# Twenty small loads in the middle of a cached-attention decode kernel: sixteen on GpSimd's queue, four on SP's

## The chip, the cores and the metric

The kernel runs on one core of one Trainium2 chip. The metric is the device time of one execution in microseconds (us). The engines are PE (TensorE), DVE (VectorE), ACT (ScalarE), POOL (GpSimd) and SP (SyncE, which only issues DMAs here). Transfers issued by SP, ACT and POOL are carried by the core's 16 DMA engines.

## The reference

Everything is fp32. One new token for each of two batch rows attends over a cache of 4096 keys and values in 16 heads of 256; beside it a small feed-forward network runs on the same token, and a gate mixes the two:

```python
g = sigmoid((x * gate_w).sum(-1, keepdims=True))      # x: (2, 1, 448)
q = (x @ wq).reshape(B, 1, 16, 256).transpose(0, 2, 1, 3)
p = softmax(einsum("bhqd,bhkd->bhqk", q, k_cache) * 256 ** -0.5)
a = einsum("bhqk,bhkd->bhqd", p, v_cache).transpose(0, 2, 1, 3).reshape(B, 1, 4096) @ wo
h = relu(x @ w1 + b1)
b = (h * h) @ w2 + b2                                  # w1: (448, 1792)
return g * a + (1 - g) * b
```

The two caches, 2 x 16 x 4096 x 256 x 4 B = 134 MB each, are nearly all of the data.

## The kernel before

The attention is cut into 16 rounds (`rounds`, L258): a round is two heads of one batch row. For a round, K and V come as 128 partitions of 64 rows of 256, 8.39 MB each (`of_round`, L264): a partition holds 64 consecutive keys of one head.

**Buffers.** K has two tiles, `kp0` and `kp1`, used in turn by round (`load_k`, L268). V has one, `vp` (`load_v`, L272). All three also take other things at other times: `wq` and `w1` pass through `vp` at the start, the output weights `wo` through `kp` after each group of four rounds (`load_wo`, L514), and `w2` through `kp1` at the end.

**A round's work.** DVE multiplies the K tile in place by the query (`times_q`, L399, recorded at L403) and sums each 256 (`row_sums`, L405, recorded at L408) into the scores `s0` or `s1`, in turn by round. `rest` (L411) does both for the two halves of the tile: product, sum, product, sum. `maximum` (L418) and `softmax` (L427) make the weights with DVE, PE and ACT. `values` (L465) multiplies them with V on PE into the PSUM tile `po0`. After four rounds `sums`, `norm`, `turn_wide` and `project` bring the group's output through `wo` into `acc`.

**Order.** The program is written out by hand as one list of operations. `Flow.op` (L46) takes, with every operation, the regions that it reads (`r`) and writes (`w`), and puts it at the end of its engine's queue. An operation that reads a region waits for the last that wrote it; one that writes a region waits for those that wrote or read it before. A wait that is already implied by what the engine has waited for is left out (`know`). A DMA counts on a semaphore of its own name, stands in the queue of the engine that issues it, and counts as having read or written its regions when it has landed. An engine works its queue in order, so a wait holds all that stands behind it on that engine.

`load` (L251) records a DMA. Thus SP's queue in round i is: V of round i (waits until `values(i - 1)` has read `vp`), then K of round i + 2 (waits until DVE has summed the K tile of round i), and, after each fourth round, `wo`. The main loop is at L575 to L600:

```python
for i in range(LOOPED):          # LOOPED = 12
    ...
    vt = load_v(i, vp)
    if i < last - 3 - 1 or i + 2 < 14:
        load_k(i + 2)
    values(i, vt)
    clear(i)
    rest(i + 1, 0, 0)
    ...
    maximum(i + 1, True)
    softmax(i + 1)
```

Rounds 12 to 15 follow, written out one by one (L602 to L650), then the last products with `wo` and `w2` into `fin` (L652 to L655), a copy by ACT (L657) and the two stores (L659, L660). At the end SP clears the kernel's semaphores (L168).

POOL makes the identity matrix at the start (L298, L299) and a few constants, and issues no DMA. ACT issues four small loads at the start (L291 to L294) and one of the two stores.

Of the kernel before, what the change touches and what calls it, by code (L numbers as in the profile page):

```python
# [10 lines left out]
PE, ACT, DVE, POOL, SP = "PE", "ACT", "DVE", "POOL", "SP"  # L11
# [159 lines left out]
def gated_mix_kernel(nc, x, k_cache, v_cache, wq, wo, w1, b1, w2, b2, gate_w, out):  # L171
    P = 128
    B, H, S, DH = k_cache.shape
# [30 lines left out]
    def sb(name, *shape):  # L204
        return nc.alloc_sbuf_tensor(name, shape, F32).ap()
# [42 lines left out]
    def rows(t):  # L248
        return t.rearrange("p (j d) -> p j d", d=DH)

    def load(eng, sem, dst, src, w, r=(), give=None):  # L251
        e = flow.eng[eng]
        op(eng, lambda: e.dma_start(dst, src), r=r, w=w, dma=sem, give=give)

    def place(t, lo=0, hi=NK * DH):
        return ("vp" if t is vp else "kp1" if t is kp[1] else "kp0", lo, hi)
# [7 lines left out]
    def of_round(src, i):  # L264
        b, n = rounds[i]
        return src[b, 2 * n:2 * n + 2].rearrange("h (p j) d -> (h p) j d", p=PH)

    def load_k(i, lo=0, hi=NK):  # L268
        t = kp[i % 2]
        load(SP, f"k{i % 2}_{lo}", rows(t)[:, lo:hi, :], of_round(k_cache, i)[:, lo:hi, :], [place(t, lo * DH, hi * DH)])  # L270

    def load_v(i, t, cuts=()):  # L272
        at = [0, *cuts, NK]
        for lo, hi in zip(at, at[1:]):
            give = "v" if i < LOOPED else None
            load(SP, "v" if give else f"v{i}_{lo}", rows(t)[:, lo:hi, :], of_round(v_cache, i)[:, lo:hi, :],
                 [place(t, lo * DH, hi * DH)], give=give)
        return t
# [50 lines left out]
    def mms(calls):  # L329
        def run():  # L330
            for out_, lhsT, rhs, start, stop in calls:
                i = t_.matmul(out_, lhsT, rhs, start=start, stop=stop, skip_group_check=True)  # L332
            return i
        return run

    op(PE, mms([(pxv[:, c, :], xr[:, c].rearrange("b r s -> b (r s)"), ident[:B, :B], True, True) for c in range(XC)]),
       r=[xr_r, "ident"], w=["sm"])
# [35 lines left out]
    def make_q(i, token=False):  # L373
        c = sel if token else col(i)
        op(PE, mms([(pq[k * PH:(k + 1) * PH, :DH], c.to_broadcast([P, PH]), qs[:, k * DH:(k + 1) * DH], True, True)
                    for k in range(2)]), r=["qs", "sel" if token else "ident"], w=["pq"], take=["q"] if token else ())
        t = q_t[i % 3]
        q_of[i] = t
        op(ACT, lambda: s_.activation(t, pq[:, :DH], AF.Copy), r=["pq"], w=[f"q{i % 3}"])  # L379

    def pick(i):
        c = col(i)
        op(ACT, lambda: s_.activation(sel, c, AF.Copy), r=["ident"], w=["sel"], give="q")
# [10 lines left out]
    for k in range(FB // 2):  # L394
        op(ACT, lambda k=k: s_.activation(h_sb[:, k * D:(k + 1) * D], ph[32 * k:32 * k + 2 * B, :D], AF.Copy),
           r=["ph"], w=[("shared", k * D, (k + 1) * D)])
    load_k(1)

    def times_q(i, half, lo, hi):  # L399
        t, a, q = kp[i % 2], half * J, q_of[i]  # L400
        kt = rows(t)[:, a + lo:a + hi, :]
        at = [place(t, (a + lo) * DH, (a + hi) * DH)]
        vec(lambda: v_.tensor_tensor(kt, kt, q.unsqueeze(1).to_broadcast([P, hi - lo, DH]), op=ALU.mult), at + [f"q{i % 3}"], at)  # L403

    def row_sums(i, half):  # L405
        t, s = kp[i % 2], s_t[i % 2]
        at = slice(half * J, (half + 1) * J)
        vec(lambda: v_.tensor_reduce(s[:, at], rows(t)[:, at, :], axis=AX.X, op=ALU.add),  # L408
            [place(t, half * HALF, (half + 1) * HALF)], [(f"s{i % 2}", half, half + 1)])

    def rest(i, first, lead):  # L411
        if lead < J:
            times_q(i, first, lead, J)
        row_sums(i, first)
        times_q(i, 1 - first, 0, J)
        row_sums(i, 1 - first)

    def maximum(i, token=False):  # L418
        s = s_t[i % 2]
        vec(lambda: v_.tensor_reduce(m, s, axis=AX.X, op=ALU.max), [f"s{i % 2}"], ["m"], give="m" if token else None)  # L420
        op(PE, mms([(mt[k * PH:(k + 1) * PH, :PH], m.to_broadcast([P, PH]), ident[:, k * PH:(k + 1) * PH], True, True)
                    for k in range(2)]), r=["m", "ident"], w=["mt"], take=["m"] if token else ())

    def buf(i):
        return 0 if i <= LOOPED else i % 2

    def softmax(i):  # L427
        b, n = rounds[i]
        s, nb, rs, pw = s_t[i % 2], nb_t[i % 2], None, pwt[buf(i)]
        vec(lambda: v_.tensor_reduce(nb, mt[:, :PH], axis=AX.X, op=ALU.max, negate=True), ["mt"], [f"nb{i % 2}"])  # L430
        u, k = unit_of[2 * n]
        rs = rs_t[u % 2]

        def part(e):
            at = slice(e * PH, (e + 1) * PH)
            c = B * (k + e) + b
            op(ACT, lambda: s_.activation(pw[at, :, 2 * c:2 * c + 2], s[at].rearrange("p (m s) -> p m s", s=2), AF.Exp,  # L437
                                          bias=nb[at], accum_out=rs[at, c:c + 1]),
               r=[f"s{i % 2}", f"nb{i % 2}"], w=[(f"pw{buf(i)}", 2 * c, 2 * c + 2), (f"rs{u % 2}", c, c + 1)],
               give="pw" if e and i < LOOPED else None)  # L440

        part(0)
        part(1)

    def clear(i):
        b, n = rounds[i]
        u, k = unit_of[2 * n]
        at = pwt[0].rearrange("p m (k b s) -> p m k b s", b=B, s=2)[:, :, k:k + 2, b, :]
        op(ACT, lambda: s_.activation(at, zero.unsqueeze(2).unsqueeze(3).to_broadcast([P, NK // 2, 2, 2]), AF.Copy), r=["zero"],  # L449
           w=[("pw0", 2 * (B * (k + e) + b), 2 * (B * (k + e) + b) + 2) for e in range(2)])  # L450

    def sums(u):
        n = B * len(units[u])
        op(PE, mms([(sm[:, :n], ones_pp, rs_t[u % 2][:, :n], True, True)]), r=["ones", f"rs{u % 2}"], w=["sm"])
# [10 lines left out]
    def values(i, vt, lo=0, hi=NK // 2):  # L465
        b, h = rounds[i]
        u, k = unit_of[2 * h]
        n = len(units[u])
        po, pw = po_t[u % 2 if u > 2 else 0], pwt[buf(i)]
        name = f"po{u % 2 if u > 2 else 0}"  # L470
        token = i < LOOPED
        calls = []
        for mm in range(lo, hi):
            r = 32 * (mm % 4)
            calls.append((po[r:r + 4 * n, :], pw[:, mm, :4 * n], vt[:, 2 * mm * DH:(2 * mm + 2) * DH],
                          not token and k == 0 and b == 0 and mm < 4,
                          token or (k == n - 2 and b == B - 1 and mm >= NK // 2 - 4)))
        op(PE, mms(calls), r=[f"pw{buf(i)}", place(vt, 2 * lo * DH, 2 * hi * DH)], w=[name], take=["pw", "v"] if token else ())
# [35 lines left out]
    def load_wo(u, i):  # L514
        t = kp[i % 2]
        tv = t[:, :HJ * D]
        if u < NG - 1:
            load(SP, "wo", tv, wo_g[u], [place(t, 0, HJ * D)])
        else:
            load(SP, "wo3", tv.rearrange("p (h k) -> p h k", h=HG), wo_v[:, u * HG:(u + 1) * HG, :], [place(t, 0, HJ * D)])  # L520
# [38 lines left out]
    def ffn_square(pt):  # L559
        for a in range(2):  # L560
            at = slice(a * PH, (a + 1) * PH)
            vec(lambda a=a, at=at: v_.tensor_tensor(hb[at], pt[at, :, a * B:(a + 1) * B], b1T[at].unsqueeze(2).to_broadcast([PH, FC, B]),
                                         op=ALU.add), ["sm", "b1T"], [("hb", a, a + 1)])
        vec(lambda: v_.tensor_scalar(hb, hb, 0.0, None, op0=ALU.max), ["hb"], ["hb"])
        vec(lambda: v_.tensor_mul(hT, hb, hb), ["hb"], ["hT"])
        vec(lambda: v_.tensor_tensor(hT, hT, gP[:, 1, :].unsqueeze(1).to_broadcast([P, FC, B]), op=ALU.mult), ["hT", "gP"], ["hT"])
# [5 lines left out]
    make_q(2)  # L572
    pick(3)

    for i in range(LOOPED):  # L575
        if i % HG == 0:
            flow.loop()
        flow.next_pass()
        vt = load_v(i, vp)
        if i < last - 3 - 1 or i + 2 < 14:  # L580
            load_k(i + 2)
        values(i, vt)
        clear(i)
        rest(i + 1, 0, 0)
        if i == 0:
            ffn_square(pt)
        if i % HG == HG - 1:
            load_wo(i // HG, i + 1)
        maximum(i + 1, True)
        softmax(i + 1)  # L590
        make_q(i + 3, True)
        if i < LOOPED - 1:
            pick(i + 4)
        if i % HG == HG - 1:
            u = i // HG
            flow.end_loop(16 * u)
            sums(u)
            norm(u)
            turn_wide(u)
            project(u)  # L600

    i = last - 3  # L602
# [16 lines left out]
    i = last - 2  # L619
# [13 lines left out]
    i = last - 1  # L633
# [55 lines left out]
```

## Time and profile before

| | us |
|---|---|
| median of 3 runs | 678.31 (678.14 to 678.61) |
| the profiled execution | 678.43 |
| its span, first to last instruction | 677.1 |
| DVE busy | 569.6 (84%) |
| PE busy, matmuls | 246.3 (36%) |
| PE busy, weight loads | 83.3 (12%) |
| ACT busy | 42.6 (6%) |
| POOL busy | 0.7 (6 instructions) |

Times inside the profile are counted from the span's start. The page cuts the span into 40 equal slices and gives for each the busy tenths of the DMA engines and what they moved. Queues are numbered: q1 is fed by SP, q10 by ACT, q8 and q14 fetch instructions. A row of a group gives line, engine, operation, output and input, count, then busy time and mean ns of one, then the idle time just before them and what ended it. SPq is SP's queue of DMA issues; the time of such a row is that of issuing, not of the transfer.

### The profile page before, as it was taken

To read this page: it belongs to the slowest core of one execution; us is meant where nothing else is said; L and a number is where in the kernel's file an instruction comes from. 1 tells how busy PE (TensorE), PEld (TensorE's weight loads), DVE (VectorE), ACT (ScalarE), POOL (GpSimd) and SP (SyncE) were. 2 spreads that over 40 slices of the span, in tenths; PEclk is the share of its full clock that TensorE was granted. 3 is DMA by queue.
4 is the path that set the end of the run, shared out by engine and by line. 5 is a ranking of instruction groups with operands and counts; after the bars stand their busy time and mean duration, and the time that the engine had idled before them with its cause. 6 is when DMAs were issued, how large, how long until landed. Compare 5 with 4: busy or idle time off the path is not lost.

```text
span 677.1 us, 3790 instructions
## 1 busy us (share of the span) xinstructions
PE 246.3 (36%) x1658; PEld 83.3 (12%) x1658; DVE 569.6 (84%) x141; ACT 42.6 (6%) x142; POOL 0.7 (0%) x6
## 2 busy tenths in 40 slices
PE   2522350502306751140505455040411580602486
PEld 1100210100101510010101411010100240100122
DVE  3069999999999895979979896997979899999920
ACT  0001000000100201010000201000010110100000
POOL 0000000000000000000000000000000000000000
PEclk9957575665757566575856578585565865855789
DMA  9999999999999999999999999999999999999997
GB/s 380 434 430 435 435 434 434 434 434 434 434 434 434 451 434 434 434 434 434 434 434 434 430 431 434 434 434 434 434 434 434 406 451 422 432 443 434 401 429 299
DMA packets 7622, 289.71 MB, mean 428 GB/s; under 512 B 950, under 2 KB 1084, under 8 KB 2364
## 3 DMA queue, kind: packets, MB, share of 16 engines
q1 hardware_dynamic: 7448, 289.54, 99.2%
q8 instruction: 8, 0.13, 0.1%
q10 hardware_dynamic: 164, 0.02, 0.0%
q14 instruction: 2, 0.02, 0.0%
HBM read 289.56 MB, written 0.00 MB: 428 GB/s over the span
## 4 chain that ended last, share of the span: by engine, by line
DVE 41%; DMA 36%; PE 0%; issue 0%; ACT 0%; DVEq 0%
DMA kp<-in_A_k_cache_dram 32%; DVE s L408 21%; DVE kp L403 20%; DMA kp<-in_B_w_dram 4%; PE fin L332 0%; PE mt L332 0%; DVE nb L430 0%; ACT shared L657 0%; DVE rc L460 0%; DVE rl L461 0%; DVE rc L459 0%; DVE m L420 0%; DVEq L147 0%
## 5 line engine op out<-in xcount | busy, mean ns | idle before, releaser
L403 DVE TENSOR_TENSOR kp<-kp,q 128x8192 f32<-128x8192 f32 (+2 forms) x34 | 278.2, 8182 | 57.3 <-DMA kp<-in_A_k_cache_dram 57.3
L408 DVE TENSOR_REDUCE s<-kp 128x32 f32<-128x8192 f32 x32 | 277.9, 8686 | 1.1
L332 PE MATMUL po<-vp,pw 128*16 128x512 f32 (+1 forms) x960 | 138.8, 736 | 223.9 <-PEq L145 207.1
L332 PEld LDWEIGHTS po<-vp,pw 128*16 128x16 f32 (+1 forms) x960 | 31.1, 111 | 327.4 <-issue 306.4
L332 PE MATMUL mt<-ident,m 128*64 128x64 f32 x64 | 7.3, 318 | 148.9 <-PEq L145 85.5
L332 PE MATMUL sm<-rl,shared 128*128 128x8 f32 (+1 forms) x112 | 23.6, 347 | 9.1 <-ACT shared L488 8.1
L332 PE MATMUL acc<-kp,oTw 128*2 128x448 f32 x48 | 24.3, 673 | 2.5 <-ACT oTw L497 2.5
L332 PEld LDWEIGHTS mt<-ident,m 128*64 128x64 f32 x64 | 4.8, 191 | 162.9 <-issue 97.4
L449 ACT ACTIVATE pw<-zero 128x128 f32<-128x128 f32 x12 | 3.7, 311 | 326.9 <-PE po L332 326.9
L332 PEld LDWEIGHTS sm<-rl,shared 128*128 128x128 f32 x112 | 23.0, 311 | 10.7 <-DVE rl L461 4.6
L437 ACT ACTIVATE pw<-s,nb 64x64 f32<-64x64 f32 x32 | 11.1, 348 | 176.7 <-DVE nb L430 176.5
L332 PE MATMUL ph<-vp,xT 128*4 128x448 f32 x28 | 7.2, 679 | 16.6 <-DMA vp<-in_B_w_dram 16.6
L332 PE MATMUL po<-kp,pw 128*8 128x512 f32 x64 | 10.1, 790 | 8.1 <-DMA kp<-in_A_v_cache_dram 8.1
L430 DVE TENSOR_REDUCE nb<-mt 128x1 f32<-128x64 f32 x16 | 3.6, 223 | 11.1 <-PE mt L332 11.1
L332 PE MATMUL pq<-qs,sel 128*64 128x256 f32 x48 | 12.3, 594 | 0.0
L332 PE MATMUL po<-vp,xT 128*4 128x512 f32 x56 | 7.7, 711 | 4.9 <-DMA vp<-in_A_wq_dram 4.9
L459 DVE RECIPROCAL rc<-sm 128x8 f32<-128x8 f32 (+1 forms) x5 | 1.0, 196 | 7.9 <-PE sm L332 7.9
L488 ACT ACTIVATE shared<-po 128x512 f32<-128x512 f32 x12 | 6.5, 591 | 11.4 <-PE sm L332 11.4
L379 ACT ACTIVATE q<-pq 128x256 f32<-128x256 f32 x16 | 6.1, 384 | 13.1 <-PE pq L332 12.8
L332 PEld LDWEIGHTS acc<-kp,oTw 128*2 128x2 f32 x48 | 4.5, 98 | 20.1 <-issue 17.3
L437 ACT ACTIVATION_READ_ACCUMULATOR pw<-s,nb 64x1 f32 x32 | 5.9, 185 | 0.0
L332 PEld LDWEIGHTS pq<-qs,sel 128*64 128x64 f32 x48 | 4.1, 212 | 0.0
(64 smaller groups left out, 61.9 us busy)
## 6 DMA issues: line engine op xcount, KB each, us to landing
kp<-in_A_k_cache_dram SPq DMA_DIRECT2D x4, 4096.0 KB, 27.5
vp<-in_A_wq_dram SPq DMA_DIRECT2D x1, 7168.0 KB, 19.7
kp<-in_A_wo_dram SPq DMA_DIRECT2D x4, 1792.0 KB, 25.5
vp<-in_A_v_cache_dram SPq DMA_DIRECT2D x1, 4096.0 KB, 24.1
vp<-in_B_w_dram SPq DMA_DIRECT2D x1, 3136.0 KB, 19.0
vp<-in_A_v_cache_dram SPq DMA_DIRECT2D x1, 2048.0 KB, 28.6
kp<-in_B_w_dram SPq DMA_DIRECT2D x2, 896.0 KB, 29.9
vp<-in_A_v_cache_dram SPq DMA_DIRECT2D x1, 1024.0 KB, 30.6
```

The source lines that it names most:

```text
L332: i = t_.matmul(out_, lhsT, rhs, start=start, stop=stop, skip_group_check=True)
L379: op(ACT, lambda: s_.activation(t, pq[:, :DH], AF.Copy), r=["pq"], w=[f"q{i % 3}"])
L403: vec(lambda: v_.tensor_tensor(kt, kt, q.unsqueeze(1).to_broadcast([P, hi - lo, DH]), op=ALU.mult), at + [f"q{i % 3}"], at)
L408: vec(lambda: v_.tensor_reduce(s[:, at], rows(t)[:, at, :], axis=AX.X, op=ALU.add), [place(t, half * HALF, (half + 1) * HALF)], [(f"s{i % ...
L430: vec(lambda: v_.tensor_reduce(nb, mt[:, :PH], axis=AX.X, op=ALU.max, negate=True), ["mt"], [f"nb{i % 2}"])
L437: op(ACT, lambda: s_.activation(pw[at, :, 2 * c:2 * c + 2], s[at].rearrange("p (m s) -> p m s", s=2), AF.Exp, bias=nb[at], accum_out=rs[at ...
L449: op(ACT, lambda: s_.activation(at, zero.unsqueeze(2).unsqueeze(3).to_broadcast([P, NK // 2, 2, 2]), AF.Copy), r=["zero"], w=[("pw0", 2 * ...
L459: vec(lambda: v_.reciprocal(c, sm[:, :B * n].rearrange("p (k b) -> p k b", b=B)), ["sm"], ["rc"])
L488: op(ACT, lambda s=s, lo=lo: s_.activation(o_w[:, s], pv[:, s, lo:lo + HJ // 2].unsqueeze(2).to_broadcast([P, HJ // 2, HG, HP]), AF.Copy), ...
```

## The change

Two spare tiles of 8 partitions by 4 x 256 elements are allocated, one for SP's small loads and one for POOL's. A new function `few` loads the first `k` partitions' first four rows of a round's K cache, `k` rows of 4 KB, into the spare tile, and names the scores of that round as read. In the rounds 2 to 9 POOL issues two such loads of one row; in the rounds 4 to 7 SP issues one of 1, 2, 4 and 8 rows, right after the K load of round i + 2. Nothing reads the spare tiles. Each load has a semaphore of its own. Since all loads of one engine write the same tile, each waits until the one before it has landed; since they name the scores as read, the sum that next writes those scores (round i + 2, or i + 3 for the loads called `two`) waits until they have landed. [...]

```diff
+    spare = {e: sb(f"spare{e}", 8, 4 * DH) for e in (SP, POOL)}
+
+    def few(eng, name, k, i):
+        load(eng, name, spare[eng][:k], of_round(k_cache, i)[:k, :4, :].rearrange("p j d -> p (j d)"), [f"spare{eng}"],
+             r=[f"s{i % 2}"])
+
     for i in range(LOOPED):
         if i % HG == 0:
             flow.loop()
@@
         vt = load_v(i, vp)
         if i < last - 3 - 1 or i + 2 < 14:
             load_k(i + 2)
+        if 2 <= i < 10:
+            few(POOL, f"one{i}", 1, i)
+        if 4 <= i < 8:
+            few(SP, f"few{i}", 1 << i - 4, i)
         values(i, vt)
         clear(i)
         rest(i + 1, 0, 0)
+        if 2 <= i < 10:
+            few(POOL, f"two{i}", 1, i + 1)
         if i == 0:
             ffn_square(pt)
@@
-    nc = _bacc.Bacc("TRN2", target_bir_lowering=False, num_devices=1)
+    nc = _bacc.Bacc("TRN2", target_bir_lowering=False, num_devices=1, dynamic_dma_scratch_size=8192)
```

## The prediction

> **What bounds the kernel now.** I read the page's slices and queues first, because the loads added are DMA work. In the slices each digit is a fortieth of the span.
>
> ```profile
> span 677.1 us, 3790 instructions
> DMA  9999999999999999999999999999999999999997
> GB/s 380 434 430 435 435 434 434 434 434 434 434 434 434 451 434 434 434 434 434 434 434 434 430 431 434 434 434 434 434 434 434 406 451 422 432 443 434 401 429 299
> DMA packets 7622, 289.71 MB, mean 428 GB/s; under 512 B 950, under 2 KB 1084, under 8 KB 2364
> q1 hardware_dynamic: 7448, 289.54, 99.2%
> q8 instruction: 8, 0.13, 0.1%
> q10 hardware_dynamic: 164, 0.02, 0.0%
> ```
>
> The 16 DMA engines are busy from start to end, and q1, which SP feeds, takes 99.2% of them. Slice after slice moves 434 GB/s; a sixteenth of that, 27.1 GB/s, is one engine's rate. 289.71 MB at 434 GB/s are 667.5 us of the 677.1. So the kernel is a DMA queue that never runs dry: whatever adds time to the DMA engines adds it to the end, and whatever delays another engine adds nothing until SP issues so late that the queue empties.
>
> How full is the queue? First the issues (KB each if alike, median us from issue to landing), then SP's own order, the K-cache and V-cache loads around the rounds that the change touches.
>
> ```profile
> kp<-in_A_k_cache_dram SPq DMA_DIRECT2D x14, 39.3
> vp<-in_A_v_cache_dram SPq DMA_DIRECT2D x14, 29.6
> ```
>
> ```profile
> 212.61 0.33 SPq L253 DMA_DIRECT2D vp<-in_A_v_cache_dram  x1
> 239.60 0.33 SPq L253 DMA_DIRECT2D kp<-in_A_k_cache_dram  x1
> 256.40 0.33 SPq L253 DMA_DIRECT2D vp<-in_A_v_cache_dram  x1
> 257.13 0.33 SPq L253 DMA_DIRECT2D kp<-in_A_k_cache_dram  x1
> 294.53 0.33 SPq L253 DMA_DIRECT2D vp<-in_A_v_cache_dram  x1
> 300.33 0.33 SPq L253 DMA_DIRECT2D kp<-in_A_k_cache_dram  x1
> 332.66 0.33 SPq L253 DMA_DIRECT2D vp<-in_A_v_cache_dram  x1
> ```
>
> A round's K or V is 2 heads x 4096 x 256 x 4 B = 8.39 MB, 19.3 us at 434 GB/s. A K load lands 39.3 us after its issue, so some 20 us of other loads are ahead of it; a V load has 10 us ahead.
>
> VectorE (DVE) is the second engine. Its rows, and its order in one stretch:
>
> ```profile
> L403 DVE TENSOR_TENSOR kp<-kp,q 128x8192 f32<-128x8192 f32 (+2 forms) x34 | 278.2, 8182 | 57.3 <-DMA kp<-in_A_k_cache_dram 57.3
> L408 DVE TENSOR_REDUCE s<-kp 128x32 f32<-128x8192 f32 x32 | 277.9, 8686 | 1.1
> ```
>
> ```profile
> 182.73 0.22 DVE L420 TENSOR_REDUCE m<-s 128x1 f32<-128x64 f32 x1
> 231.09 8.69 DVE L408 TENSOR_REDUCE s<-kp 128x32 f32<-128x8192 f32 x1
> 257.13 0.22 DVE L420 TENSOR_REDUCE m<-s 128x1 f32<-128x64 f32 x1
> 265.57 8.69 DVE L403 TENSOR_TENSOR kp<-kp,q 128x8192 f32<-128x8192 f32 x1 [7.47 <-DMA kp<-in_A_k_cache_dram]
> 274.30 8.69 DVE L408 TENSOR_REDUCE s<-kp 128x32 f32<-128x8192 f32 x1
> 304.34 8.69 DVE L403 TENSOR_TENSOR kp<-kp,q 128x8192 f32<-128x8192 f32 x1 [2.90 <-DMA kp<-in_A_k_cache_dram]
> ```
>
> ```profile
> DVE 41%; DMA 36%; PE 0%; issue 0%; ACT 0%; DVEq 0%
> ```
>
> A round is four operations of 8.7 us and waits for its K load: 7.47 us before round 6, 2.90 before round 7. The chain of waits puts 41% of the span on DVE and 36% on DMA, but it follows semaphores: it names DVE because DVE frees the K buffer, while the engines behind q1 were moving an earlier load. The full DMA row decides.
>
> **The change part by part.** Nothing is removed. Added are twenty loads with twenty semaphores of their own, 16 x 1 + 1 + 2 + 4 + 8 = 31 rows of 4 KB, 127 KB, which is 0.29 us at 434 GB/s if it spreads evenly. [...]
>
> *What a small packet costs a busy engine.* At the start ACT's b1 load (128 rows of 56 B) ran between the 57,344 B pieces of wq on q1. The stretch from 2.5 to 19.5 us (40 slices of 0.425 us; packets stand at their starts), then the one from 670 to 677 (slices of 0.175 us):
>
> ```profile
> GB/s 270 0 0 0 944 1079 135 0 0 945 1089 135 0 0 945 1080 135 0 0 945 1089 135 0 0 945 1080 135 0 0 945 1080 135 0 0 945 1080 135 0 0 1081
> q10 hardware_dynamic: 111, 0.01, 0.5%
> ```
>
> ```profile
> DMA  8898999999675544411000000000000000000000
> q10 hardware_dynamic: 8, 0.00, 0.1%
> ```
>
> 111 packets took 0.5% of 16 x 17 us = 272 us, so 12 ns each; the 8 of the end 0.1% of 112 us, 14 ns. And they leave no gap beside themselves: with some 7 of them on each engine, the bursts of wq come every 5 slices, 2.125 us, and a burst looks like the one before. A piece of 57,344 B at 27.1 GB/s takes 2.116 us. So changing between two queues costs a packet's own time, some 10 ns, and no more. I price a short packet at 16 ns (12 to 14 rounded up, since 256 B are more than 56 B: 256 B at 27.1 GB/s are 9 ns), and a 4 KB packet at 4096 / 27.1 = 151 ns plus 16 ns for its completion, 167 ns.
>
> *The sixteen loads of GpSimd.* No row of before has a load on GpSimd's queue, and none has a load of one row. From the lower side, a row that goes whole to one engine and to another engine each time puts one load on each: 0.17 us. From the upper side, whole rows always on the same engine put 16 x 167 ns = 2.7 us on it. Between them, a row cut in 16 pieces of 256 B puts two short packets, data and completion, on each engine: 16 x 2 x 16 ns = 0.51 us on all of them. I take 0.51: a contiguous row can be cut anywhere, and it lies nearer to the lower end, where the price comes from rows. [...]
>
> *The four loads of SP.* The 164 packets of q10 are 2 + 2 + 2 + 128 + 4 = 138 rows of ACT's five loads, and the 26 left over are 2 + 2 + 2 + 16 + 4: a load of k rows, k under 16, has k completions, so k engines. Then the loads of 2, 4 and 8 rows put 167 ns a row on as many engines: 3 x 167 = 0.50 us on an engine that is in all three, nothing on one in none, and 14 x 167 / 16 = 0.15 on the average. The load of one row is 0.03 cut in pieces, 0.17 whole. Issuing costs SP 0.33 us each, as its rows show, in stretches in which it waits tens of us.
>
> *Who sets the end.* The DMA row of the end falls from 9 to 1 over some 2 us: the engines finish that far apart, because each has carried its own share of instruction fetches (q8). After the last landing nothing changes:
>
> ```profile
> 673.71 0.95 PE L332 MATMUL fin<-kp,hT 128*2 128x112 f32 x32 [0.67 <-DMA kp<-in_B_w_dram]
> 674.72 0.26 ACT L657 ACTIVATE shared<-fin 128x112 f32<-128x112 f32 x1 [5.03 <-PE fin L332]
> 675.01 0.64 SPq L253 DMA_DIRECT2D out_dram<-shared  x1
> ```
>
> If the last engine carries none of SP's rows, the end moves by GpSimd's part alone.
>
> *The waits, all covered.* (1) SP's second to fourth small load wait for the one before to land (the same spare tile), which is behind a K load in q1. At i = 5 SP has issued K of round 7 at 257.13 and then stands until that of round 6 has landed, about 265.6; queued behind it on SP is V of round 6, due at 294.53, so 29 us are left. At i = 6 it stands from 300.7 to about 304.3, and V of round 7 is due at 332.66. The wait for the scores is no wait: the K load just ahead on SP has already waited for that sum. If this cover were gone, a delay D would cost D less the loads still queued: K at 239.60 landed by 265.57, 26.0 less 19.3, so 6.7 us are the thinnest cushion of this stretch. (2) DVE's first sum of round i + 2 overwrites the scores that the small loads name as read, so it waits for up to three landings. GpSimd's loads of round 3's scores are released at 182.7 and needed at 231.09: 48 us. SP's land right behind the K load of round i + 2, and the sum comes one product, 8.7 us, later. 274.30 comes 0.04 us after the end of the operation at 265.57, waits included; three more waits at that price are 0.12 us a round, and DVE idles 2.9 us or more for K in these rounds. (3) GpSimd has nothing else queued after its six instructions at the start.
>
> Sum: 0.51 + 0.03 + 0.15 = 0.7 us. The profiled execution took 678.43 us (span 677.1, 1.3 around it), 0.12 over the median of 678.31; so 679.1 from the one, 679.0 from the other. I predict **679.0**. The bounds of the unknown prices are 678.31 + 0.17 = 678.5 and 678.31 + 2.7 + 0.50 + 0.17 = 681.7.
>
> **The rivals.** *Rows whole on one engine (slower).* If a one-row load isn't cut, and GpSimd always begins at the same engine, that engine has 2.7 us of its own, plus 0.67 where it also carries SP's. Bulk loads are complete when their slowest engine is, and the end waits for it. It decides from the point at which the extra exceeds that engine's lead over the last one, at most the 2 us of the DMA row above. For it: ACT's two-row loads did use just two engines. Against it: nothing but that a contiguous row can be cut. It gives 681.0 to 681.7.
>
> *GpSimd's packets hold an engine longer (slower).* If those descriptors cost not 16 ns but 100, 32 of them on each engine are 3.2 us: 681.5. For it: no row shows that queue. Against it: q10, the other small queue, leaves no gap. A stronger form: a small load occupies all 16 engines for a fixed span, whatever its bytes. If a load held them for half a microsecond or more, 20 loads would be 10 us and above, 688 and later. The packets of q10 speak against it, since 111 of them took 1.4 us in all. [...]
>
> *A wait that isn't covered (slower).* A small load that lands 45 us late would hold DVE. Nothing in the rows comes near.
>
> [...]
>
> **How the numbers follow.** 0.2% is 1.36 us, about what a measurement of this kernel can tell from no change. Forecast, 678.2 to 679.6, within 0.2%: 0.65. Rows whole on one engine: 0.13. GpSimd's packets dearer: 0.12. Fixed span per load: 0.04. An uncovered wait: 0.03. Faster by over 0.2%: 0.03. So slower is 0.32, the same 0.65, faster 0.03. The range goes from 678.2 (the lower bound less the 0.3 by which runs of before spread) to 681.7, the upper bound; outside are the fixed span, the uncovered wait, the fast case and part of the dearer packets, under 0.2.
>
> **What would show it.** Right: a new queue with 16 x 32 = 512 packets, mostly under 512 B, at a share of 0.1% or less; the GB/s row still at 434; DVE's idle time before L408 unchanged; SP's V issues no later than before by more than the drift of under 1 us. If rows go whole, the new queue has some 4 KB packets and the DMA row of the end falls more slowly, one engine trailing. If GpSimd's packets are dearer, GB/s falls below 434 between 147 and 500 us, and nowhere else. A wait of DVE for a spare tile, or a gap in the DMA row, would make the whole argument wrong.

## The result, and the profile after

The changed kernel takes 682.33 us (median of 4 runs, 682.09 to 682.44) against 678.30: 4.0 us more, ratio 1.0059 with a 95% interval of 1.0047 to 1.0071. The profiled execution took 682.43 us. From its page: span, what each fortieth of it moved, the queues, and DVE's two large groups.

```profile
span 681.1 us, 3831 instructions
GB/s 378 466 423 444 440 435 431 431 431 431 431 424 408 453 431 428 435 432 431 431 433 431 449 432 431 427 435 431 431 435 431 416 444 421 431 445 435 406 419 225
q1 hardware_dynamic: 7478, 289.60, 98.7%
q0 software_dynamic: 512, 0.07, 0.1%
L403 DVE TENSOR_TENSOR kp<-kp,q 128x8192 f32<-128x8192 f32 (+2 forms) x34 | 278.2, 8183 | 61.8 <-DMA kp<-in_A_k_cache_dram 61.8
L408 DVE TENSOR_REDUCE s<-kp 128x32 f32<-128x8192 f32 x32 | 278.0, 8686 | 1.1
```

Much is as before. GpSimd's queue (q0) has 512 packets that take 0.1%; q1 has 30 packets more, 15 rows and 15 completions. DVE waits for no small load (the 1.1 us before L408 stand), only 4.5 us longer for K. So the K loads themselves land later. The last slice moves 225 GB/s in place of 299: something drains more slowly. The end shows it, cut in slices of 0.275 us from 670 to 681 us, first the kernel before, then the changed one:

```profile
GB/s 404 384 437 358 384 431 261 254 209 209 143 65 33 13 0 0 0 0 0 0 0 0 7 7 0 0 0 0 0 0 0 0 0 0 0 0 0 0 0 0
```

```profile
GB/s 437 417 417 417 391 372 450 358 235 319 222 215 248 117 52 26 26 26 86 26 39 20 20 39 20 20 26 26 0 0 0 0 0 0 0 0 0 7 7 0
```

27.1 GB/s, a sixteenth of the 434 of the full slices, is the rate of one DMA engine. Before, the rate falls from that of 16 engines to none within some 2 us. After, most engines end about half a microsecond later than before, and then 13 slices, 3.6 us, run at 20 to 39 GB/s (q8's one packet here, a 16 KB instruction fetch, makes the 86): **one engine works on alone.** The last product waits for it; before, the same row stood at 673.71:

```profile
677.69 0.95 PE L332 MATMUL fin<-kp,hT 128*2 128x112 f32 x32 [0.69 <-DMA kp<-in_B_w_dram]
```

SP's queue, in the stretch that the prediction showed, and its waits for small loads in all:

```profile
257.24 0.33 SPq L253 DMA_DIRECT2D kp<-in_A_k_cache_dram  x1
266.12 0.25 SPq L253 DMA_DIRECT2D spareSP<-in_A_k_cache_dram  x1
295.08 0.33 SPq L253 DMA_DIRECT2D vp<-in_A_v_cache_dram  x1
300.70 0.33 SPq L253 DMA_DIRECT2D kp<-in_A_k_cache_dram  x1
305.21 0.27 SPq L253 DMA_DIRECT2D spareSP<-in_A_k_cache_dram  x1
333.60 0.33 SPq L253 DMA_DIRECT2D vp<-in_A_v_cache_dram  x1
```

```profile
SPq L253 <- DMA spareSP<-in_A_k_cache_dram: 17.7, 3, 8.5
```

SP stands as predicted, 8.5 us at most, and the V loads follow when they did, later by 0.55 and 0.94 us, within the drift that was allowed.

### The profile page after: what moved, and what is told of

Same layout as the page of the kernel before. It is cut to its first block, busy times and chain, and to the rows that moved or that the text cites. A ratio compares the mean times of both kernels' runs of the same rounds, so it can differ in the third digit from the quotient of the medians.

```text
span 681.1 us, 3831 instructions
## 1 busy us (share of the span) xinstructions
PE 244.9 (36%) x1658; PEld 83.0 (12%) x1658; DVE 569.8 (84%) x141; ACT 42.6 (6%) x142; POOL 8.6 (1%) x22
## 4 chain that ended last, share of the span: by engine, by line
DVE 41%; DMA 37%; PE 0%; issue 0%; ACT 0%; DVEq 0%
DMA kp<-in_A_k_cache_dram 33%; DVE s L408 20%; DVE kp L403 20%; DMA kp<-in_B_w_dram 4%; PE fin L332 0%; PE mt L332 0%; DVE nb L430 0%; ACT shared L669 0%; DVE rc L460 0%; DVE rl L461 0%; DVE rc L459 0%; DVE m L420 0%; DVEq L147 0%
## 5 line engine op out<-in xcount | busy, mean ns | idle before, releaser
L408 DVE TENSOR_REDUCE s<-kp 128x32 f32<-128x8192 f32 x32 | 278.0, 8686 | 1.1
L332 PE MATMUL po<-vp,pw 128*16 128x512 f32 (+1 forms) x960 | 135.8, 722 | 232.0 <-PEq L145 215.5
L253 POOL DMA_DIRECT2D sparePOOL<-in_A_k_cache_dram x16 | 7.9, 493 | 455.0 <-DVE s L408 401.4
```

## The experiments

**Theory A**: the pieces of a row come from 16 engines and all land in one partition of SBUF; the engine that brings the bulk rows of that place is held, that is, its own packets take longer. **B**: the upkeep of GpSimd's queue holds one engine, whatever the data. **C**: SP's whole rows pile up on one engine. That a row's pieces come from sixteen engines is read off the packet records of the changed kernel: those of the first load start between 151.7 and 152.9 us, and their completions, taken in order, follow by 2.43 to 2.63 us. In between, sixteen bulk packets of 64 KB start, of 2.42 us each (median), so sixteen engines are at work at once. Times are medians; each is set against the runs of the kernel before that were made with it (678.3 to 678.4).

| kernel | us | over before | ratio, 95% interval |
|---|---|---|---|
| GpSimd's sixteen alone, partition 0 | 680.88 | 2.50 | 1.0020 to 1.0049 |
| SP's four alone | 678.95 | 0.57 | 0.9997 to 1.0017 |
| GpSimd's, 16 partitions in turn | 679.04 | 0.66 | 1.0000 to 1.0019 |
| GpSimd's, 256 B a row | 678.73 | 0.35 | 0.9995 to 1.0014 |
| GpSimd's, 8 KB a row | 683.00 | 4.62 | 1.0051 to 1.0085 |
| whole change, GpSimd's rows in partition 64 | 680.25 | 1.87 | 1.0017 to 1.0039 |
| GpSimd's, partitions 0-3 and 32-35 in turn | 680.73 | 2.35 | 1.0022 to 1.0047 |
| whole change, each row over 16 partitions | 679.58 | 1.20 | 1.0008 to 1.0027 |
| sixteen cut rows through SP, partition 0 | 680.64 | 2.30 | 1.0021 to 1.0046 |
| the same through GpSimd, no wait between loads | 680.76 | 2.42 | 1.0023 to 1.0048 |
| sixteen whole rows through SP, partition 0 | 679.41 | 1.07 | 1.0006 to 1.0025 |
| thirty-two through GpSimd, no wait between loads | 684.51 | 6.15 | 1.0074 to 1.0107 |

### Each part alone

```diff
-        if 4 <= i < 8:
-            few(SP, f"few{i}", 1 << i - 4, i)
```

> GpSimd's sixteen loads alone, SP's four left out. The changed kernel's trace shows one DMA engine trailing the others at the end, by 5.9 us where the last trailed by 2.2 before. Theory A (all pieces of a one-row load land in one partition of SBUF, and the engine that carries the bulk rows of that place is held, some 0.3 us a load): 681.6, with the trailing engine still there. Theory B (upkeep of GpSimd's queue holds one engine, whatever the data are): also 681.6. Theory C (SP's whole rows pile up on one engine): 678.8.

```diff
-        if 2 <= i < 10:
-            few(POOL, f"one{i}", 1, i)
...
-        if 2 <= i < 10:
-            few(POOL, f"two{i}", 1, i + 1)
```

> SP's four loads alone, GpSimd's sixteen left out. A and B: at most 0.7 us above before, 678.3 to 679.0, and no long trail at the end. C: 681.6 or more.

680.88 and 678.95. C falls as the main cause: SP's rows alone cost 0.57, hardly more than the runs spread. GpSimd's loads alone cost 0.7 us less than the 681.6 that A and B gave, but they leave the trail, from slice 14 to 22 of the same stretch (counted from 0):

```profile
GB/s 437 437 417 424 372 391 378 261 254 241 189 183 203 65 20 20 39 20 20 39 13 26 13 0 0 0 0 0 0 0 0 5 7 2 0 0 0 0 0 0
```

The parts make 2.50 + 0.57 = 3.1, together 4.0. That fits two delays of the same engine of which each, taken alone, is partly hidden by that engine's lead: the time by which it would have ended before the last engine. A and B are both still open.

### The place, and the bytes

```diff
-    spare = {e: sb(f"spare{e}", 8, 4 * DH) for e in (SP, POOL)}
+    spare = {SP: sb("spareSP", 8, 4 * DH), POOL: sb("sparePOOL", P, 4 * DH)}
+    turn = [4 * (n % 8) + PH * (n // 8) for n in range(16)]
...
+        p = turn.pop(0) if eng == POOL else 0
+        load(eng, name, spare[eng][p:p + k], of_round(k_cache, i)[:k, :4, :].rearrange("p j d -> p (j d)"), [f"spare{eng}"],
```

(SP's four are left out in this and the next two.)

> GpSimd's sixteen loads alone, each into another partition: 0, 4, 8 to 28 and 64, 68 to 92. Queue, bytes, packets and waits are those of the kernel with GpSimd's loads alone. A: each engine is held at most once or twice, 678.6 to 679.2, no engine trails alone. B: 681.6, the same engine trails as with one partition.

```diff
-        load(eng, name, spare[eng][:k], of_round(k_cache, i)[:k, :4, :].rearrange("p j d -> p (j d)"), [f"spare{eng}"],
+        load(eng, name, spare[eng][:k, :64], of_round(k_cache, i)[:k, 0, :64], [f"spare{eng}"],
```

> GpSimd's sixteen loads alone, a row of 64 elements in place of 1024 (16 pieces of 16 B), still into partition 0. A: the held time goes with the bytes, so 678.4 to 678.9. B: packets and upkeep are the same, 681.6.

679.04 and 678.73, both within A's ranges and far from the 681.6 of B: B is out. In the first of the two, queue, packets, waits and source rows are those of GpSimd's loads alone; only the partition differs, and the lone engine is gone:

```profile
GB/s 391 437 411 384 417 417 339 398 418 248 293 163 196 137 59 20 0 0 0 0 0 0 0 0 2 7 5 0 0 0 0 0 0 0 0 0 0 0 0 0
q0 software_dynamic: 512, 0.07, 0.1%
```

More bytes into partition 0:

```diff
-    spare = {e: sb(f"spare{e}", 8, 4 * DH) for e in (SP, POOL)}
+    spare = {POOL: sb("sparePOOL", 8, 8 * DH)}
...
-        load(eng, name, spare[eng][:k], of_round(k_cache, i)[:k, :4, :].rearrange("p j d -> p (j d)"), [f"spare{eng}"],
+        load(eng, name, spare[eng][:k], of_round(k_cache, i)[:k, :8, :].rearrange("p j d -> p (j d)"), [f"spare{eng}"],
```

> GpSimd's sixteen loads alone, rows of 8 KB (16 pieces of 512 B) into partition 0, against rows of 4 KB (680.9) and of 256 B (678.7). A, with a hold of one engine that goes with the bytes: some 0.27 us a load at 4 KB becomes 0.45 to 0.55, so 683.5 to 685.0. If the hold were per load and only absent for very small pieces: 680.9.

683.00, half a microsecond under the range expected: the hold grows with the bytes, but less than in proportion. (With the engine's lead of 1.3 us, found below, 8 KB cost an estimated (4.62 + 1.3) / 16 = 0.37 us a load, against 0.23 for 4 KB.)

### One engine, and which partitions are its own

```diff
+    spare = {SP: sb("spareSP", 8, 4 * DH), POOL: sb("sparePOOL", P, 4 * DH)[PH:PH + 8]}
```

> The whole change, but GpSimd's rows go to partition 64 in place of 0; SP's stay in partitions 0 to 7. GpSimd's loads alone cost 2.5 us, SP's alone 0.6, both 4.0. A: both parts of the change hold the same engine, the one with the bulk rows of partitions 0 to 3; moved to partition 64, GpSimd's rows hold another engine, and the end is the later of the two, 680.6 to 681.2. Rival: the two parts add up on whatever engine is last (a queue matter, not a matter of place): 682.3.

680.25: below A's range by 0.35, and 2.1 below the same twenty loads with partition 0. So the place counts for the two parts together as well. Whether they still add in part isn't settled, since GpSimd's rows in partition 64 alone were not run: an engine there with a longer lead would show less of the same hold.

```diff
+    turn = [n % 4 + 32 * (n // 4 % 2) for n in range(16)]
```

(the rest as for the 16 partitions in turn)

> GpSimd's sixteen loads alone, in turn into partitions 0, 1, 2, 3, 32, 33, 34, 35. [...] If what matters is the one partition, or eight partitions in a row: the hold is on two engines or more, 678.8 to 679.8.

680.73, as with partition 0 alone, where eight partitions of several engines would have shared the hold. The engine trails alone from slice 14 to 21:

```profile
GB/s 397 411 489 339 391 372 463 248 228 254 189 163 104 99 39 20 39 20 20 26 26 20 0 0 0 0 0 0 0 0 0 7 7 0 0 0 0 0 0 0
```

So writes into partitions 0 to 3 and 32 to 35 hold one engine: 680.73 here, 680.88 with partition 0 alone, and 679.04 with sixteen partitions in turn.

The packet records of the traces show the hold itself. The median 64 KB packet of a bulk load takes 2.42 us, and an engine starts its next packet as one ends (q1 alone fills 98.9% of the sixteen engines' span in this run). So the packets can be strung into sixteen chains, though the trace names no engine and where two end together the chain is a guess. In this run the 64 KB packets of one chain lose 3.6 us in all against that median, those of any other 0.9 at most; in the kernel before 1.0 is the most, and with the 16 partitions in turn 1.2. The twenty slow packets of that chain, 2.48 to 2.68 us, all lie between the first small load and the last.

### The queue, the waits, and the price of a load

```diff
+    spare = sb("spare", 8, 3 * 16 * 65)
+    slot = [n % 3 for n in range(16)]
...
+        n = slot.pop(0)
+        dst = spare[:1, n * 1040:(n + 1) * 1040].rearrange("p (e x) -> p e x", x=65)[:, :, :64]
+        load(SP, name, dst, of_round(k_cache, i)[:1, :4, :].rearrange("p j (e x) -> p (j e) x", e=4), [f"spare{n}"],
...
+            few(SP, f"one{i}", 1, i)
...
+            few(SP, f"two{i}", 1, i)
```

> No GpSimd load at all: the sixteen rows of 4 KB go through SP's queue, each cut by hand in 16 pieces of 256 B into partition 0 (three places in turn, so that SP hardly waits), issued right behind the K loads. A: what counts is that 16 engines write one partition, whatever queue they are fed from, so one engine is held as with GpSimd's loads: 680.4 to 681.2. Rival D: GpSimd's queue is needed for the hold (its descriptors or their timing): 678.7 to 679.2.

The same with `load(eng, ...)`, issued by GpSimd where the change issues its loads:

> The same pieces and places as in the kernel that sends sixteen cut rows through SP, but through GpSimd's queue; against GpSimd's loads alone it lacks only the wait of each load for the one before (three places in turn). A: 680.9 as with the wait, since the waits cost nothing. If the waits had a part in the 2.5 us: 678.7 to 680.2.

680.64 and 680.76. D is out, GpSimd's queue has no part in it: without any load on it the cost is the same, and in the first of the two its row is gone from the queues:

```profile
q1 hardware_dynamic: 7960, 289.61, 99.0%
```

7960 is 7448 + 512. The waits of one small load for another cost nothing either. (These kernels and the two that follow also give the change's last argument, `dynamic_dma_scratch_size`, another value, 1024 through SP and 2048 through GpSimd in place of 8192; 680.76 against 680.88 shows no effect of it.)

```diff
+        load(SP, name, spare[:1, n * 1024:(n + 1) * 1024], of_round(k_cache, i)[:1, :4, :].rearrange("p j d -> p (j d)"), [f"spare{n}"],
```

> Sixteen rows of 4 KB through SP's queue, uncut, into partition 0: one packet of 4 KB each, on one engine. A: the engine that carries them writes its own place and is charged 0.167 us a row, 2.7 us in all, which is hidden as far as that engine led the last one (2.0 us or so): 678.8 to 679.6, and the other engines lose nothing. If cutting makes no difference, 680.9.

679.41: uncut, the same bytes in the same place cost 1.07 us in place of 2.3.

Back to GpSimd's cut rows without waits, now thirty-two:

```diff
+            few(POOL, f"three{i}", 1, i)
...
+            few(POOL, f"four{i}", 1, i + 1)
```

> Thirty-two loads of one row through GpSimd's queue in place of sixteen, otherwise as the kernel with three places in turn (680.8). The held engine is then last from the first sixteen on, so the second sixteen show the price of a load undiminished by its lead. A: 0.21 us a load if that engine led by 0.9 us, 0.26 if by 1.6, so 684.1 to 684.9. If the price saturates or is hidden: below 682.5.

684.51. The second sixteen cost 3.75 us, **0.23 us a load**, with no lead left to hide them. The first sixteen showed 2.42, so if they cost as much, the engine of partition 0 led the last one by 3.75 - 2.42 = 1.3 us. With that lead the uncut rows cost an estimated (1.07 + 1.3) / 16 = 0.15 us each, just what 4 KB take at 27.1 GB/s.

### All twenty, spread

```diff
+    spare = {e: sb(f"spare{e}", P, 4 * DH) for e in (SP, POOL)}
...
+        row = of_round(k_cache, i)[:k, :4, :].rearrange("p j (e x) -> (j e) p x", e=4)
+        dst = spare[eng][0:P:8, :k * 64].rearrange("e (p x) -> e p x", p=k)
+        load(eng, name, dst, row, [f"spare{eng}"], r=[f"s{i % 2}"])
```

> All twenty loads with the same bytes, but each row laid as 16 pieces of 256 B into 16 partitions (0, 8, 16 to 120); SP's rows are thereby cut in 16 as well. A: the hold is spread over at least eight engines, 678.8 to 679.4, no engine trails alone at the end. B (upkeep of GpSimd's queue) is already out; if small pieces cost by themselves, SP's 240 pieces in place of 15 rows would bring it to 681 or more.

679.58: 2.8 us of the change's 4.0 are gone with the same bytes through the same queues, but it is 0.2 above the range expected. No engine trails alone; all of them end later:

```profile
GB/s 443 417 404 450 384 398 456 358 378 404 392 248 196 209 163 130 72 7 0 0 0 0 0 0 0 0 7 7 0 0 0 0 0 0 0 0 0 0 0 0
```

The work has not vanished, it is shared: by the prediction's price an engine carries 16 x 32 ns for GpSimd's loads and 19 x 16 ns for SP's (15 pieces, 4 completions), 0.81 us. The holds come on top, an estimated (3.75 + 1.5) / 16 = 0.33 if all sixteen engines share them, and 0.66 if only eight do; how many do was not shown. That makes 1.1 to 1.5, against 1.20 measured. No version beats the kernel before, which has none of these loads.

## Why the prediction was wrong

679.0 was predicted, within 0.2%, with a range up to 681.7; 682.33 was measured.

**The step that failed** is the price of GpSimd's sixteen loads, "data and completion, on each engine: 16 x 2 x 16 ns = 0.51 us on all of them". The trace of before has no load of one row, so no run showed the cut in 16 or the sixteen completions of that term; in the changed kernel q0 has 256 packets of 256 B and 256 completions of 4 B. Its count was right (512 packets) and so was the price of a packet on the engine that carries it (the packet records have 18 ns for 256 B and 9 ns for a completion, where 16 was taken for each). What it left out is where they land. Sixteen engines write the same partition, and one engine's bulk packets take longer meanwhile (2.48 to 2.68 us in place of 2.42, with partitions 0 to 3 and 32 to 35), far beyond the one piece in sixteen that it carries. That it is the engine that brings that partition's bulk rows is inferred from the eight partitions that share the hold, since the trace names no engine. What the trace of before could show about small packets was b1, whose 128 rows of 56 B go to 128 partitions, one row to each, so its even period said nothing of sixteen rows in one partition. Measured in the step's place: 0.23 us a load on one engine, 3.75 us for sixteen, of which its lead hid 1.3.

**SP's four loads** were taken at 0.03 + 0.15 on the average engine. Alone they cost 0.57, with an interval that takes in both nothing and a full microsecond, so the 0.18 is neither shown nor refuted. In the whole change they cost 682.33 - 680.88 = 1.5 us, since they land in partitions 0 to 7, so 11 of their 15 rows in partitions 0 to 3, the place that GpSimd's rows also hold. If the engine of that place carries the first row of each load, those four make 4 x 0.167 = 0.67 of that; the rest would be held time from the seven rows that other engines write there. No run tried either by itself. The one-row load was not cut on SP: q1's 30 new packets, 15 rows and 15 completions, leave no room for 16 pieces. The cut in 16 held for GpSimd alone.

**Who sets the end** was half right. The prediction saw that an extra counts only on the last engine, and allowed the last engine to carry none of SP's rows; it did not see that the extras would pick one engine and make it the last. The lead that the rival spoke of is there: 1.3 us. That the engines end some 2 us apart because of their shares of instruction fetches was not tested by any run.

**The rival "rows whole on one engine"** gave the picture, one engine trailing, and nearly the time, but not the cause: GpSimd's rows were cut. It was put at 681.7 at most, by carriage alone. "GpSimd's packets hold an engine longer" is out: the same pieces cost 2.3 us through SP's queue. The fixed span per load, 10 us and more, is out as well: all twenty cost 4.0 us.

**The waits** were right: SP stood 8.5 us at most and 17.7 in all, DVE waited for no small load, and taking the waits between GpSimd's loads away changed nothing (680.76 against 680.88).

**The range** failed because its upper end, 2.7 + 0.50 + 0.17, summed what an engine carries. No bound was set on what it loses to others' writes, though the destination, partition 0 sixteen times, stood in the diff.

## What to carry to other kernels

Where the DMA engines are busy from start to end, as here, the end belongs to the last of sixteen, so a small load is priced by where it lands as well as by what carries it: ask which engine brings the bulk rows of that partition. The scratch rows that always went to partition 0 all charged the same engine; laid over 16 partitions, the sixteen loads cost 0.66 us in place of 2.50. In the profile the sign is a trail at the end at the rate of one engine (here 20 to 39 GB/s, with 27.1 for one engine).

## What the runs showed of the hardware

- A cut row written into one partition by 16 engines costs one engine 0.23 us for 4 KB (3.75 us for sixteen), more than the 0.15 us that 4 KB take at its own 27.1 GB/s. A row uncut, on SP's queue, cost less (1.07 in place of 2.30 us for sixteen). Why the cut row costs more than its bytes stays open; the runs show that it goes with the place and grows with the bytes (0.35 us for sixteen rows of 256 B, 2.50 for 4 KB, 4.62 for 8 KB).
- A one-row load of 4 KB is 16 pieces on GpSimd's queue (q0 has 512 packets for sixteen loads, 256 pieces of 256 B and 256 completions) and one packet on SP's (sixteen whole rows bring q1 from 7448 to 7480 packets, a row and a completion each).
- Writes into partitions 0 to 3 and 32 to 35 charge the same engine (680.73 us, with partition 0 alone 680.88); partition 64 is another's (the whole change takes 680.25 with GpSimd's rows there, 682.33 with them in partition 0).
- Delays of loads that land in the same place add up: sixteen more into partition 0 took 680.76 to 684.51 us.
